# Two raw quads moved into an idle activation buffer, and a newly searched instruction order, in a fused linear-attention and MLP kernel

## The chip, the cores and the metric

One core of a Trainium2 chip. The metric is the device time of one execution in microseconds (us). Runs of one kernel on one chip scatter by 1 to 2 us in either direction, so a difference of 1 us is only seen over several runs of both kernels on the same chip.

## The reference

```python
def phi(x):                                   # x: 8 batches, 8 heads, 576 positions, 64 channels
    proj = einsum('bhsd,md->bhsm', x, omega)  # omega: 128 x 64
    return concatenate([cos(proj), sin(proj)], axis=-1) / sqrt(m)
q_p, k_p = phi(q), phi(k)
kv  = einsum('bhsm,bhsd->bhmd', k_p, v);  z = sum(k_p, axis=2)
num = einsum('bhsm,bhmd->bhsd', q_p, kv); den = einsum('bhsm,bhm->bhs', q_p, z)
x = (num / den), heads side by side           # 8 x 576 x 512
u = x + ((x^T @ U) @ V)^T                     # low rank, over the positions
out = u + relu(u @ w_ch1) @ w_ch2             # 512 -> 2048 -> 512
```

Inputs and output are float32. The kernel computes in bf16 with float32 sums.

## The kernel before

The 64 heads are taken as 16 "quads" of four heads and as 32 "groups" of two. Each head pair's k and q are loaded (`ld/k/n`, `ld/q/n`), transposed (on TensorE for quads 0 to 3: `tpp`, copied out by `tp`, which is called the eviction; by a transposing DMA, also `tp`, for the later quads), multiplied by omega (`ak`, `aq`), turned into table angles on VectorE (`uk`, `uq`), into sines and cosines on ScalarE (`s`, `c`, with a quarter-turn `p` between them on GpSimd), then into `kv` (TensorE, copied by `kvb`), numerators (`num`) and the normalised `x`. The MLP products are `w1` and `w2`. v is loaded (`ldv`) and widened to bf16 on GpSimd (`wv`).

Every instruction is a word of one long list; each engine executes its own words in the order of the list.

```python
rawp = ctx.enter_context(tc.tile_pool(name="rawp", bufs=2))     # two quads of raw k and q
hidp = ctx.enter_context(tc.tile_pool(name="hidp", bufs=2))     # two MLP activation buffers
low_f = hidp.tile([P, NFT, SM], BF16, name="hid")...bitcast(F32)  # the second one, unused until batch 1,
Vf  = low_f[:, 0:S]                                             # is where U and V are staged
U_f = low_f[:, S:S + NS * R]...
# ...
add("gate", DVE, lambda: nc.vector.memset(low_f[:, S - 1:S + NS * R], 0.0))
add("low", SP, load_low_rank, needs=["gate"])                   # four DMAs
add("lowc", POOL, cast_low_rank, needs=["low"])
# ...
def load_w1(a):                                                 # a quarter of W1: 512 KB
    nc.gpsimd.dma_start(W1b[:, a, :, :], moe_w_ch1[:, a * 512:(a + 1) * 512]...)
# ...
    need = [r for r in read_raw(name, n - NRAW)] if n >= NRAW else []   # NRAW = 2
    add(("ld", name, n), POOL, lambda ...: nc.gpsimd.dma_start(load(name, n), quad(src, n)), needs=need)
# ...
    add(("ldv", n), SP if n else POOL, load_v, needs=[("wv", n - 2)] if n >= 2 else [])
    add(("wv", n), POOL, widen, needs=["begin", ("ldv", n)] + ...)
```

The part of the order, with cuts:

```
... ukh/0/1 aq/0@4 d/8@6 gate skh/0/0 uq/0 d/9@7 low ... pk/0 tpp/k/1@6 uk/1 ... ldv/1 pq/0 tp/k/1 d/11@1
aq/1@1 tp/q/1 ld/q/2 cq/0 uq/1 ak/2@3 wv/0 aq/2@6 uk/2 d/12@1 s/1 W1/0 ldv/2 kv/0/0@0 ld/k/3
uq/2 ak/3@2 W1/1 kv/0/1 p/1 ... p/2 num/0 tp/k/2 tp/q/2 d/13@2 sk/3 x/0 ak/4@5 ld/q/3 wv/1 ...
```

## Time and profile before

| | before |
|---|---|
| time, median of 4 fast runs | 358.88 us (358.36 to 359.5) |
| span of the profiled run | 358.0 us |
| TensorE (PE) busy | 341.3 us, 95% |
| PE idle before 30 us | 9.3 us |
| start of the first MLP product that needs W1's second piece | 39.94 us |

PE is the bound from 30 us on. A second profile of the same kernel, taken later on another chip, ends at 356.05 us; below it is "before, second profile".

### The profile page before, as it was taken

What the parts mean: (1) busy time and instruction counts of PE and PEld (TensorE: products, weight loads), DVE (VectorE), ACT (ScalarE), POOL (GpSimd) and SP (SyncE); (2) the same over time, 40 slices, a digit from 0 to 9 for tenths busy, and PEclk for the clock granted to TensorE, in tenths of its full rate; (3) what the DMA queues carried; (4) which work ended last, traced back from release to release, by engine and by line L of the source; (5) the groups of instructions that cost most, each with busy time, mean ns of one, the idle gap of its engine ahead of it and who ended that gap; (6) DMA issues with size and microseconds to landing.
All of it is one profiled execution on the core that took longest, in us unless ns stands there. A gap on an engine that the chain in (4) does not pass through costs nothing.

```text
span 358.0 us, 8213 instructions
## 1 busy us (share of the span) xinstructions
PE 341.3 (95%) x3544; PEld 180.4 (50%) x3585; DVE 193.2 (54%) x284; ACT 216.8 (61%) x223; POOL 117.3 (33%) x100
## 2 busy tenths in 40 slices
PE   7659999999999999989999999999999999999996
PEld 3446456454564554645455554554545544444444
DVE  3968868786687676866476754364320722000111
ACT  5868899559958877678829578437386004553210
POOL 5879185427634536324704043003230000000000
PEclk9869999999999999999999999999999999999999
DMA  8997989999999886999992086200722051511124
GB/s 173 224 239 116 203 142 195 217 178 227 192 194 192 123 246 128 115 177 166 196 183 46 3 212 140 62 3 0 148 60 44 2 104 29 117 31 29 37 53 88
DMA packets 68567, 45.06 MB, mean 126 GB/s; under 512 B 47156, under 2 KB 59828, under 8 KB 68532
## 3 DMA queue, kind: packets, MB, share of 16 engines
q1 hardware_dynamic: 55348, 30.09, 41.2%
q0 software_dynamic: 12816, 13.93, 25.5%
q8 instruction: 28, 0.46, 0.5%
q10 hardware_dynamic: 368, 0.52, 0.4%
q14 instruction: 7, 0.06, 0.1%
HBM read 37.16 MB, written 9.44 MB: 130 GB/s over the span
## 4 chain that ended last, share of the span: by engine, by line
PE 88%; DMA 7%; ACT 1%; issue 1%; POOL 1%; POOLq 0%
PE ps L610 35%; PE ps L630 34%; PE ps L430 5%; PE ps L444 4%; DMA raw<-in_q_dram 4%; DMA T<-raw 3%; PE ps L381 2%; PE ps L407 2%; PE ps L576 2%; PE ps L449 1%; PE ps L514 1%; ACT ft L416 1%; PE ps L321 1%; POOL ang L420 1%; PE ps L584 0%
## 5 line engine op out<-in xcount | busy, mean ns | idle before, releaser
L416 ACT ACTIVATE ft<-ang 128x2304 bf16<-128x2304 int16 (+2 forms) x67 | 134.1, 2020 | 35.4 <-DVE ang L359 15.3
L630 PE MATMUL ps<-W2b,hid 128*128 128x512 bf16 (+1 forms) x560 | 130.5, 373 | 2.6 <-issue 1.4
L623 ACT ACTIVATE hid<-ps 128x512 bf16<-128x512 f32 x144 | 81.9, 596 | 84.4 <-PE ps L610 83.9
L610 PE MATMUL ps<-uT,W1b 128*128 128x512 bf16 x512 | 121.7, 379 | 0.8 <-DMA uT<-u 0.6
L420 POOL TENSOR_SCALAR ang<-ang 128x2304 int32<-128x2304 int32 (+2 forms) x34 | 67.9, 2000 | 126.2 <-ACT ft L416 119.4
L359 DVE TENSOR_SCALAR ang<-ps 128x1280 int32<-128x1280 f32 (+2 forms) x66 | 84.8, 1313 | 24.7 <-PE ps L375 16.3
L630 PEld LDWEIGHTS <-hid 128*128 128x128 bf16 x592 | 55.4, 98 | 62.0 <-issue 2.1
L610 PEld LDWEIGHTS <-W1b 128*128 128x128 bf16 x576 | 54.3, 98 | 63.8 <-issue 1.4
L646 DVE TENSOR_TENSOR o<-ps,u 128x512 f32<-128x512 f32 x32 | 21.9, 686 | 52.1 <-PE ps L630 52.0
L430 PEld LDWEIGHTS <-ft 64*128 64x128 bf16 x1152 | 24.1, 96 | 9.9 <-issue 5.7
L430 PE MATMUL ps<-vq,ft 64*128 64x65 bf16 x1152 | 27.1, 193 | 1.4 <-DVE ang L359 0.9
L460 DVE TENSOR_TENSOR x<-ps,rec 128x640 bf16<-128x640 f32 x32 | 26.4, 825 | 1.1
L434 DVE CAST kvb<-ps 128x260 bf16<-128x260 f32 x32 | 13.4, 423 | 20.6 <-PE ps L430 19.8
L578 DVE TENSOR_TENSOR u<-ps,x 128x1024 bf16<-128x1024 f32 x16 | 19.2, 1221 | 9.6 <-PE ps L610 4.9
L305 POOL CAST vq<-vraw 128x1152 bf16<-128x1152 f32 x16 | 18.5, 1153 | 12.1 <-DMA vraw<-in_v_dram 12.1
L444 PEld LDWEIGHTS <-ft 128*128 128x128 bf16 x512 | 19.9, 99 | 5.0 <-issue 0.5
L444 PE MATMUL ps<-kvb,ft 128*128 128x65 bf16 x512 | 21.9, 195 | 0.0
L610 PE MATMUL ps<-utailT,W1b 128*128 128x512 bf16 x64 | 15.1, 379 | 0.0
L458 DVE RECIPROCAL ps<-ps 128x10 f32<-128x10 f32 x32 | 7.2, 224 | 13.8 <-PE ps L449 13.3
L381 PE MATMUL ps<-WT,T 64*128 64x128 bf16 x256 | 13.5, 222 | 1.1 <-DMA T<-raw 0.6
L298 POOL DMA_DIRECT2D raw<-in_k_dram x15 | 10.9, 725 | 10.2 <-ACT hid L623 6.3
L407 PE MATMUL ps<-T,WT 64*128 64x512 bf16 x64 | 13.2, 387 | 0.0
(58 smaller groups left out, 150.7 us busy)
## 6 DMA issues: line engine op xcount, KB each, us to landing
out_dram<-o SPq DMA_DIRECT2D x70, 128.0 KB, 2.4
vraw<-in_v_dram SPq DMA_DIRECT2D x15, 576.0 KB, 5.7
raw<-in_k_dram POOLq DMA_DIRECT2D x15, 288.0 KB, 5.7
raw<-in_q_dram POOLq DMA_DIRECT2D x15, 288.0 KB, 6.0
W1b<-in_moe_w_ch_dram POOLq DMA_DIRECT2D x4, 512.0 KB, 9.9
W2b<-in_moe_w_ch_dram POOLq DMA_DIRECT2D x4, 512.0 KB, 8.9
vraw<-in_v_dram POOLq DMA_DIRECT2D x1, 576.0 KB, 7.5
ang<-in_q_dram ACTq DMA_DIRECT2D x1, 288.0 KB, 3.5
```

The lines of the kernel that those rows point to most:

```text
L359: nc.vector.tensor_scalar(out=dst, in0=src, scalar1=TO_UNITS, scalar2=None, op0=ALU.mult)
L381: nc.tensor.matmul(pk[:, e, i * P:(i + 1) * P], kT[r, c, :], WT[r, :])
L407: nc.tensor.matmul(pq[:, e, :], WT[r, :], transposed("q", n)[r, c:c + 4, :])
L416: nc.scalar.activation(out=held["ft", g].rearrange("p f a c -> p f (a c)")[:, f, lo:hi], in_=low[:, lo:hi, 0], func=ACT.Sin, scale=TO_RAD)
L420: nc.gpsimd.tensor_scalar(out=ang, in0=ang, scalar1=TURN / 4.0, scalar2=1.0, op0=ALU.add, op1=ALU.mult)
L430: nc.tensor.matmul(kv_ps[:, hh, o], ft[r, f, 0, c:c + M], vq[n % NV][r, NS * (g % 2) + s, :], start=(s == 0), stop=(s == NS - 1))
L444: nc.tensor.matmul(nd[:, hh, t, :], ft[:, f, 1, c:c + P], kvb[:, hh, f, :], start=(f == 0), stop=(f == 1))
L460: nc.vector.tensor_tensor(out=x[:, :, hp * P:(hp + 1) * P].rearrange("p t (h d) -> p h t d", h=2), in0=nd[:, :, :, 0:D], in1=rec.unsqueeze ...
L610: nc.tensor.matmul(one(key), W1b[:, f // 4, ct, f % 4 * P:(f % 4 + 1) * P], uT[:, :, ct, :], start=(ct == 0), stop=(ct == NCT - 1))
L623: nc.scalar.activation(out=held["hid", b][:, f, :], in_=one(at_bank), func=ACT.Relu)
L630: nc.tensor.matmul(one(key)[:, 0:cs.stop - cs.start], held["hid", b][:, f, t * P:(t + 1) * P], W2b[:, f, cs], start=(f == 0), stop=(f == N ...
L646: nc.vector.tensor_tensor(out=held["o", b, t][:, cs], in0=one(key)[:, 0:cs.stop - cs.start], in1=u[:, t, cs], op=ALU.add)
```

## The change

The stated intent: keep the first two raw quads in the second MLP activation buffer, so that the loads of quads 2 and 3 need not wait for the transposes of quads 0 and 1, and search the whole order again with later transfers assumed late and with loads kept apart from DMA transposes.

```diff
+    low_h = hidp.tile([P, NFT, SM], BF16, name="hid").rearrange("p f t -> p (f t)")
+    low_f = low_h.bitcast(F32)
+    early_raw = [low_h[:, 2 * (S + NS * R) + n * 4 * NS * D:...].rearrange(...) for n in range(2)]
...
-            held["raw", n] = rawp.tile([P, 2, 2, NS * D], BF16, name="raw")
+            held["raw", n] = early_raw[n] if n < 2 else rawp.tile([P, 2, 2, NS * D], BF16, name="raw")
...
-                need = [r for r in read_raw(name, n - NRAW)] if n >= NRAW else []
+                need = [r for x in "kq" for r in read_raw(x, n - NRAW)] if n >= NRAW + 2 else []
...  (batch 1's activations wait for the transposes of quads 0 and 1)
```

The order, cut (the new one; all other words move as well):

```
begin first/k/0 first/k/1 ident first/q/0 om ld/k/0 ... ld/q/0 d/2@5 ldv/0 ... ld/k/1 ... ld/q/1 ... ld/k/2 ... W1/0
... ld/q/2 ... wv/0 skh/0/0 ukh/0/1 ... ld/k/3 ld/q/3 ... pk/0 ... tp/k/1 tpp/k/2@0 tp/q/1 pq/0 d/10@5 gate tp/k/2
ak/2@5 low ... ldv/1 kv/0/1 ldv/2 ... p/1 num/0 tp/q/2 x/0 p/2 c/1 aq/3@0 ak/4@5 uq/3 aq/4@2 ld/k/4 ... lowc
... ld/q/4 uk/5 sq/3 pk/3 ... x/1 d/12@5 wv/1 ... pq/3 ck/3 ldv/3 kv/2/0@0 ... wv/2 ... p/4 ... x/3 ut0/0 ut0x/1@0 ut0/1 W1/1
```

## The prediction

> **What bounds the kernel now.** I read the busy table first, then the 40 slices, the chain that ended last, the waits of each engine in the first 40 us, and a table of windows.
>
> ```profile
> PE 341.3 (95%) x3544; PEld 180.4 (50%) x3585; DVE 193.2 (54%) x284; ACT 216.8 (61%) x223; POOL 117.3 (33%) x100
> PE   7659999999999999989999999999999999999996
> PEclk9869999999999999999999999999999999999999
> DMA  8997989999999886999992086200722051511124
> PE 88%; DMA 7%; ACT 1%; issue 1%; POOL 1%; POOLq 0%
> ```
>
> TensorE (PE) is the bound, at nine tenths or more in every slice (8.95 us each) but the first three, one in the middle and the last. The change does not alter the number of matmuls, so time can come only from PE's lost time, 358.0 - 341.3 = 16.7 us idle, plus what it loses at half clock. The windows place it:
>
> ```profile
> 0.00:4.57 4.57, 3.21 (x8) 1.16 (x9) 0.52 (x5) 2.24 (x4) 3.82 (x11) 1.00 0.61 160
> 4.57:14.81 10.24, 6.85 (x79) 3.67 (x78) 8.47 (x14) 6.90 (x9) 4.99 (x6) 1.00 1.05 213
> 14.81:25.05 10.24, 6.70 (x97) 5.33 (x98) 7.02 (x10) 6.68 (x4) 8.32 (x8) 0.50 1.17 235
> 25.05:30.00 4.95, 3.90 (x146) 3.25 (x142) 4.79 (x8) 4.89 (x5) 4.37 (x6) 1.00 0.76 129
> 30.00:100.00 70.00, 69.48 (x888) 37.83 (x892) 53.54 (x80) 57.48 (x56) 39.32 (x33) 1.00 1.07 187
> 100.00:200.00 100.00, 97.35 (x1213) 52.67 (x1228) 69.28 (x97) 69.28 (x61) 40.45 (x30) 1.00 0.90 156
> ```
>
> The second number is the length, the third PE's busy time, the last three the clock, the DMA share and GB/s. Before 30 us PE is idle 1.36 + 3.39 + 3.54 + 1.05 = 9.3 us, and runs 10.24 us at half clock. From 30 us on it idles 0.5 us to 100, 2.65 us to 200 and little after. So the opening is what a load change can win. In it, the chain and the waits show
>
> ```profile
> 11.84 1.20 POOL ang L420
> 13.03 8.91 DMA raw<-in_q_dram
> ...
> 21.99 1.14 PE ps L321 x9
> 23.13 0.88 PE ps L444 x16
> ...
> 24.27 3.29 ACT ft L416 x2
> PE ps L321 <- DMA raw<-in_q_dram: 3.6, 3, 2.6
> ACT ft L416 <- PE ps L449: 2.9, 1, 2.9
> ```
>
> The load of q for quad 2 is issued only at 13.03, because its raw buffer is that of quad 0, and lands 8.9 us later. PE stands before its transposes (L321), and behind them in PE's order is the first numerator (L444, L449). ScalarE (ACT) waits 2.9 us for that numerator before its next sine, and VectorE (DVE) 2.8 us for the transposes. That is the stall the change aims at.
>
> **What the Trainium skill says.** "DMA: Bandwidth & Descriptors", section "Issuing engines are not separate DMA queues": transfers started by any engine run on the same 16 DMA engines and interleave. The trace agrees: 235 GB/s and a DMA share of 1.17 while that load took 8.9 us, against 4.0 us for the quickest load of this kind. An earlier issue moves such a load ahead of others but makes no bandwidth. "TensorE: Matmul & The Clock Gate", Part 1: the clock is either half or full, and recent activity decides. The trace agrees that it is binary (0.50 or 1.00); here the half state lasted 10.24 us, longer than the 3.4 us window that the page states. The same DMA page, section "Rules for kernel authors", says to issue loads early and wait late, which is this change's idea.
>
> **The change part by part.** (a) Quads 0 and 1 go to the still unused second activation buffer, so both rotating raw buffers are free for quads 2 and 3. Their loads lose the wait for the transposes of quads 0 and 1. In exchange, batch 1's activations (r/1) wait for those transposes, which are done some 60 us before; that costs nothing. (b) GpSimd (POOL) now issues v/0 third, then quad 1, k/2, the first quarter of W1, and q/2 at once. Nine issues at about 0.72 us each from 1.44 end near 7.1, so q/2 is issued near 6.5 instead of 13.0. (c) The second quarter of W1 moves from 16.3 us to behind the quarter-turn of group 4; the low-rank loads and v/1, v/2 move behind the evictions of quad 1. (d) The evaluation of group 5 is brought forward. (e) The 20 dummy matmuls stay, but 13 instead of 16 lie in the opening, seven at the end, behind the last real matmul. (f) All the rest of the order is searched again.
>
> When does q/2 land? All bytes before it on its queue still count. Quads 0 and 1 together have 1152 KB in bf16, of which half-quads of 144 KB come from the first loads: 864 KB on this queue, then v/0 576, k/2 288, W1 512, q/2 288: 2528 KB. The busiest of the early windows moved 213 to 235 GB/s, and the first 608 KB come from other queues, so 3136 KB at about 220 KB/us from 2 us gives 16 us, plus a tail of 1 to 2 us, and some more for v/1: **17 to 19 us**, 3 to 5 us before the 21.94 of now.
>
> Is that worth 3 us? No: I walked the new order of each engine with durations of the forms in the first 40 us. DVE: angle conversions of 1280 columns 1.48 us, of 1024 columns 1.20, eviction of a half quad (1152 columns) 0.75, kv copy 0.42, normalisation 0.22 + 0.17 + 0.82. From the end of the second quarter conversion at 8.73: uk/1, ut/0, uq/0, uq/1, two evictions, the gate, one eviction, uk/2, uq/2, kvb/0 and uk/3 sum to 11.4 us, so 20.1. Then q/2's eviction, x/0, uq/3, uk/4, kvb/1, uq/4, uk/5, x/1, uq/5, kvb/2, kvb/3, k/3's eviction, two hu copies, x/2 and x/3 sum to 14.8, so x/3 ends near 34.9, or 34 as neighbouring records overlap a little. Now it ends at 34.39. So DVE, without gaps, replaces the load as the bound: x/3 comes no earlier, but the 2.7 us of group 5's conversions are done before it, and so are PE's products for group 5 (0.33 + 0.05 + 0.32 us in the chain).
>
> ACT agrees. The first quarter-turn on POOL now stands behind the widening of v/0 (1.15, after v/0 lands near 8.5 to 10) and two issues, so it starts near 11.2 instead of 9.66. The first cosine, first q sine and q cosine then end near 17, s/1 and s/2 (2.12 each) near 21, c/1 and c/2 near 25.3, against 27.6 now; sk/3, sq/3 (1.27, 1.05) near 27.6, s/4 29.7, ck/3 and cq/3 near 32, against about 31 now, but with s/4 done.
>
> PE's gain I read at the first MLP product that needs the second quarter of W1 (w1/0/4). Now it starts at 39.94. In the new order it follows x/3 by the chain of a small product, copy, product, eviction, 1.6 us, and some seven 0.22 us products: near 38. One product pair of 0.43 us, done later now, is by then done too. Gain up to 39.9 + 0.4 - 38.1 = **2.2 us**. Against it: W1's second quarter, issued near 33 behind two widenings and the quarter-turns. A quarter of W1 landed 7.6 us after issue at best in this trace, so 40 us or more. With less traffic then (that part of the trace was busy) I take 39 to 40: it gives back about 1 us. Opening: **-1.2 us**.
>
> Later: between 100 and 200 us PE waits 1.2 us for a transposing DMA (0.6 for uT, 0.6 for T). An order that keeps loads away from them may save most; I count **-0.7 us**. End: seven dummies of 0.22 us beside the last addition and store: 0. Sum: 358.8 - 1.2 - 0.7 = 356.9.
>
> **The rivals.** *The load is truly the bound, and 4 us go with it.* For: the chain gives it 8.9 us, and ACT and DVE both idle nearly 3 us behind it. Against: DVE is busy 5.00 of 5.00 us from 10 to 20, and the widening of v/0 delays ACT by a microsecond and more. Time: 354 to 355. *A new wait on weights.* For: W1's second quarter leaves its early place, and 7.6 to 12.7 us from issue to landing is measured. Against: the search was told to assume late transfers. With a 3 us wait: 358 to 360. *Loads hidden anyway, the rest saturated.* PE is at 0.99 from 30 us on, so an opening that reaches the same x/3 at the same time saves only the work done in its gaps: 357 to 358.5. *The clock.* If the half state falls after 25 us, where PE is saturated, it costs up to 5 us: 362. Against: PE does more real work in the window before, and as little activity as today's brought the full clock back at 25.05.
>
> **Range and chances.** The centre leans to the small gain of my sum: 356.8 us. The low end, 353.6, is the first rival with all middle waits gone; the high end, 360.4, a weight wait and some loss in the middle. 2% is 7.2 us: to be faster by that, three quarters of the opening's idle time would have to go; I give it 0.04. Slower by that needs a long weight wait and a half clock together: 0.02.
>
> **What would show it.** Right: the wait of L321's counterpart for q under 1 us; q/2 landing before 19.5; ACT no longer waiting 2.9 us for a numerator; DVE busy over 4.7 in each 5 us from 10 to 30; x/3 between 33.5 and 35.5; PE waiting for W1 up to 2 us near 38 to 40. Wrong: x/3 before 33 (then the load was the bound), a wait for W1 over 3 us, a half-clock stretch that reaches past 26 us, or new waits of PE for transposing DMAs after 100 us.

## The result, and the profile after

Lines of the changed kernel have numbers higher by 3: L321 became L324, L359 became L362, L416 L419, L420 L423, L444 L447, L449 L452, L610 L613.

| | before | changed |
|---|---|---|
| time, median of 4 fast runs | 358.88 us (358.36 to 359.5) | 359.99 us (359.78 to 361.01) |
| ratio | | 1.0036, 95% interval 1.0011 to 1.0061 |

A ratio is the mean time of one kernel's fast runs over that of the other's in the same rounds, so it is not quite the ratio of these medians. Five more rounds on another chip gave 1.0029 (0.9994 to 1.0063) for the changed kernel and 0.9995 for the kernel before against itself. The change costs about 1 us; a small gain had been forecast.

The busy table, PE's slices, the clock and the DMA share of the changed kernel's page, and its chain by engine:

```profile
PE 344.7 (96%) x3550; PEld 181.9 (51%) x3585; DVE 193.7 (54%) x284; ACT 218.2 (61%) x223; POOL 117.2 (33%) x100
PE   7779899999999999999999999999999999999997
PEclk9768999999999999999999999999999999999999
DMA  8998999899979996893096947432701135111124
PE 86%; POOL 4%; DMA 4%; issue 2%; DVE 1%; ACT 1%; POOLq 0%; ACTq 0%; DVEq 0%
```

In PE's row only the opening looks different; of the chain, POOL holds 4% instead of 1, and DMA 4% instead of 7. The same stretches as in the prediction, for the changed kernel:

```profile
14.81:25.05 10.24, 7.17 (x136) 5.71 (x132) 9.27 (x11) 8.78 (x5) 6.08 (x4) 0.67 1.04 225
25.05:30.00 4.95, 4.73 (x51) 2.98 (x50) 4.88 (x8) 4.95 (x5) 4.61 (x6) 0.50 0.78 123
30.00:100.00 70.00, 67.50 (x924) 37.45 (x930) 49.84 (x77) 52.30 (x52) 35.78 (x31) 1.00 1.04 184
100.00:200.00 100.00, 98.88 (x1169) 52.47 (x1179) 65.88 (x89) 72.35 (x65) 39.80 (x31) 1.00 0.76 149
```

Three things are to be seen. Before, the half clock was one stretch, 14.81 to 25.05 us, where PE was idle a third of the time. Now it is two, 13.43 to 20.26 and 23.67 to 30.50 us, and the second falls where PE is full: from 25.05 to 30 us it is busy 4.73 of 4.95 us at 0.50. From 30 to 100 us PE now lacks 2.5 us instead of 0.5. And from 100 to 200 us it lacks 1.1 instead of 2.65. PE's waits over the first 100 us:

```profile
PE ps L613 <- DMA W1b<-in_moe_w_ch_dram: 1.7, 1, 1.7
PE ps L324 <- DVE ang L362: 1.7, 3, 0.8
PE ps L384 <- DVE ang L362: 1.5, 2, 0.8
```

The wait of 2.6 us for the raw q is gone, so the change does what it was made for. A wait of 1.7 us for W1 has come. The milestones, from the starts and ends of single instructions in the traces (x/n is the end of the normalisation of group n; "ready" is the start of the first MLP product that needs W1's second piece):

| us | before | before, second profile | changed | changed, second profile |
|---|---|---|---|---|
| x/0 | 25.56 | 25.05 | 21.94 | 21.90 |
| x/1 | 30.14 | 29.63 | 29.28 | 28.93 |
| x/2 | 32.20 | 31.70 | 34.01 | 34.04 |
| x/3 | 34.39 | 33.89 | 35.20 | 35.24 |
| ready | 39.94 | 39.44 | 42.53 | 42.07 |
| end | 357.96 | 356.05 | 359.23 | 358.56 |

(Some of the expectations below count x/3 from another zero, 0.24 us earlier: their 35.5, 35.4 and 32.9 are 35.24, 35.14 and 32.62 here.)

x/0 comes 3.6 us earlier; by x/2 all of that and 2 us more is lost. From "ready" to the end three of the four profiles take nearly the same: 316.6 us (before, second), 316.7 and 316.5 (changed); the first profile of before takes 318.0, with 1.2 us of waits for transposing DMAs, which its second profile does not show. So the result is made before 43 us: +2.6 us there, and 1.3 us back in the middle, which is the stall of before that comes and goes.

### The profile page after: what moved, and what is told of

The parts are those of the page before. It is cut to its first block, busy times and chain, and to the rows that moved or that the text cites. A ratio compares the mean times of both kernels' runs of the same rounds, so it can differ in the third digit from the quotient of the medians.

```text
span 359.2 us, 8219 instructions
## 1 busy us (share of the span) xinstructions
PE 344.7 (96%) x3550; PEld 181.9 (51%) x3585; DVE 193.7 (54%) x284; ACT 218.2 (61%) x223; POOL 117.2 (33%) x100
## 4 chain that ended last, share of the span: by engine, by line
PE 86%; POOL 4%; DMA 4%; issue 2%; DVE 1%; ACT 1%; POOLq 0%; ACTq 0%; DVEq 0%
PE ps L613 34%; PE ps L633 34%; PE ps L433 5%; PE ps L447 4%; POOL ang L423 2%; DMA W1b<-in_moe_w_ch_dram 2%; PE ps L384 2%; PE ps L410 2%; DMA vraw<-in_v_dram 2%; PE ps L579 2%; ACT ft L419 1%; DVE ang L362 1%; PE ps L452 1%; PE ps L517 1%; POOL vq L308 1%
## 5 line engine op out<-in xcount | busy, mean ns | idle before, releaser
L419 ACT ACTIVATE ft<-ang 128x2304 bf16<-128x2304 int16 (+2 forms) x67 | 133.5, 2020 | 37.3 <-DVE ang L362 22.3
L633 PE MATMUL ps<-W2b,hid 128*128 128x512 bf16 (+1 forms) x560 | 132.0, 373 | 2.7 <-issue 1.6
L626 ACT ACTIVATE hid<-ps 128x512 bf16<-128x512 f32 x144 | 83.1, 597 | 74.2 <-PE ps L613 72.1
L613 PE MATMUL ps<-uT,W1b 128*128 128x512 bf16 x512 | 119.8, 379 | 1.7 <-DMA W1b<-in_moe_w_ch_dram 1.7
L423 POOL TENSOR_SCALAR ang<-ang 128x2304 int32<-128x2304 int32 (+2 forms) x34 | 67.9, 1998 | 121.0 <-ACT ft L419 111.1
L362 DVE TENSOR_SCALAR ang<-ps 128x1280 int32<-128x1280 f32 (+2 forms) x66 | 85.3, 1316 | 28.0 <-PE ps L378 13.5
L613 PEld LDWEIGHTS <-W1b 128*128 128x128 bf16 x576 | 54.6, 98 | 66.1 <-DMA W1b<-in_moe_w_ch_dram 2.2
L433 PEld LDWEIGHTS <-ft 64*128 64x128 bf16 x1152 | 22.7, 96 | 8.6 <-issue 6.5
L581 DVE TENSOR_TENSOR u<-ps,x 128x1024 bf16<-128x1024 f32 x16 | 19.4, 1222 | 13.6 <-PE ps L579 11.9
L433 PE MATMUL ps<-vq,ft 64*128 64x65 bf16 x1152 | 25.8, 194 | 0.9 <-DVE ang L362 0.7
L447 PEld LDWEIGHTS <-ft 128*128 128x128 bf16 x512 | 20.4, 100 | 5.6 <-issue 0.9
L447 PE MATMUL ps<-kvb,ft 128*128 128x65 bf16 x512 | 22.2, 197 | 0.2 <-DVE kvb L437 0.2
L410 PE MATMUL ps<-T,WT 64*128 64x512 bf16 x64 | 13.6, 393 | 1.1 <-DVE x L463 0.5
L613 PE MATMUL ps<-utailT,W1b 128*128 128x512 bf16 x64 | 14.5, 379 | 0.0
L384 PEld LDWEIGHTS <-T 64*128 64x128 bf16 x256 | 8.8, 97 | 10.4 <-issue 9.3
```

What stands on the lines that cost most here:

```text
L362: nc.vector.tensor_scalar(out=dst, in0=src, scalar1=TO_UNITS, scalar2=None, op0=ALU.mult)
L384: nc.tensor.matmul(pk[:, e, i * P:(i + 1) * P], kT[r, c, :], WT[r, :])
L419: nc.scalar.activation(out=held["ft", g].rearrange("p f a c -> p f (a c)")[:, f, lo:hi], in_=low[:, lo:hi, 0], func=ACT.Sin, scale=TO_RAD)
L423: nc.gpsimd.tensor_scalar(out=ang, in0=ang, scalar1=TURN / 4.0, scalar2=1.0, op0=ALU.add, op1=ALU.mult)
L433: nc.tensor.matmul(kv_ps[:, hh, o], ft[r, f, 0, c:c + M], vq[n % NV][r, NS * (g % 2) + s, :], start=(s == 0), stop=(s == NS - 1))
L447: nc.tensor.matmul(nd[:, hh, t, :], ft[:, f, 1, c:c + P], kvb[:, hh, f, :], start=(f == 0), stop=(f == 1))
```

## The experiments

Eighteen kernels were run, all correct. Each edits the order by moving words; a diff shows the neighbourhood. "Changed buffers" means that the new buffers are kept while the order is that of before. Ratios are to the kernel before on the same chip.

### The two kernels again

No edit.

> The kernel before, unchanged, as a measure of the noise and for a profile on the same chip as the others. Every theory: ratio 0.998 to 1.002. What is open is whether the stall of 1.4 us of PE near 155 us, which the first profile of before has behind transposing DMAs and which no variant with that order showed, is in this profile too.

> The changed kernel, unchanged, for a profile and times on this chip. Expected: 1.003 to 1.006 of before, a wait of PE for the second quarter of W1 of 1 to 2 us near 42 us, x/3 ended at 35 to 35.5.

Measured: 358.53 us, ratio 0.9995 (0.9955 to 1.0035), and 360.06 us, 1.0029 (0.9994 to 1.0063). The loss repeats in size. The stall of before in the middle does not.

### The buffers alone, and the one load alone

```diff
 # b_reloc: the new buffers, the order of before
 # b_reloc_q2: besides
-... ld/k/2 tp/q/0/0 ...   aq/1@1 tp/q/1 ld/q/2 cq/0
+... ld/k/2 ld/q/2 tp/q/0/0 ...   aq/1@1 tp/q/1 cq/0
 # b_q2_mid: ld/q/2 right behind pk/0 instead
```

> The changed kernel's buffers (quads 0 and 1 in the second activation buffer, no wait of the loads of quads 2 and 3) with the order of the kernel before. Theory (the buffers alone do nothing, as the load of q for quad 2 still stands behind two quarter-turns in GpSimd's order and is issued near 13.0): wait of L324 for q of 2 to 3 us stays, 0.998 to 1.002 of before. Rival (the wait on the buffer was itself the cause): the wait falls below 1 us and the time to 0.995 or less.

> As b_reloc, and the load of q for quad 2 issued right after that of k for quad 2 (near 5.5 us), ahead of the first quarter-turn; everything else in the order of before. Theory (the load was a real bound of this order, and the reordering of POOL and W1 is what lost its gain): q lands before 17, PE's 2.6 us and ACT's 2.9 us waits go, x/3 ends 1 to 2.5 us earlier, 0.993 to 0.997 of before. Rival (as my prediction had it, DVE is the bound as soon as the load is not): x/3 moves by less than 1 us and the time is 0.997 to 1.000 of before.

> As b_reloc_q2, but the load of q for quad 2 is issued between the two quarter-turns of group 0 (near 10.8 us, where GpSimd waits for about 1.1 us anyway) and so leaves quad 1's loads more alone. If the wait for k of quad 1 (1.9 us in b_reloc_q2, 1.0 in before) comes from the additional early load: it falls to 1.0 to 1.5 us and the time is 0 to 0.5 us below b_reloc_q2's. If q then lands too late: a wait of L324 for q of over 1 us is back and the time is 0.5 to 1 us above it.

Measured: b_reloc 357.59 us, 0.9958 (0.9919 to 0.9996); b_reloc_q2 356.40 us, 0.9925 (0.989 to 0.9959); b_q2_mid 356.32 us, 0.9942 (0.9906 to 0.9978). x/3 ends at 33.95, 32.62 and 31.81 us, the profiles at 356.11, 354.75 and 354.10.

The buffers alone leave the stall: q of quad 2 is issued at 12.76 us (12.91 in before's second profile), behind the second quarter-turn in GpSimd's order, and PE still waits 2.4 us for it. That b_reloc is 0.4% faster was not expected; its trace ends as before's second profile does (356.05), so this is not explained and may be scatter. The single load, moved into the order of before, is worth 1.3 us at x/3 against b_reloc in b_reloc_q2 and 2.1 us in b_q2_mid, and 1.4 and 2.0 us at the profiles' ends; in median time b_reloc_q2 is 1.2 us below b_reloc, and buffers and load together are 2.1 us below before. PE's wait for k of quad 1, 1.9 us in b_reloc_q2, is 0.9 in b_q2_mid, as expected; the two times cannot be told apart. **These two kernels beat the kernel before and the changed one**. So the load of q for quad 2 did set the pace of the old order. The loss comes from the newly searched order.

### The late piece of W1

```diff
 # a_w1_early, on the changed kernel
-p/2 c/1 aq/3@0 ak/4@5 uq/3 aq/4@2 ld/k/4 c/2 ...   x/3 ut0/0 ut0x/1@0 ut0/1 W1/1 ut0x/2@5
+p/2 c/1 aq/3@0 ak/4@5 uq/3 aq/4@2 ld/k/4 W1/1 c/2 ...   x/3 ut0/0 ut0x/1@0 ut0/1 ut0x/2@5
 # b_w1_late, on the kernel before: W1/1, W1/2 and W1/3 behind p/4
```

> The changed kernel with one word of its order moved: the second quarter of the first MLP weight (W1/1) is issued right after the load of k for quad 4 (near 24.3 us) instead of after the quarter-turn of group 4 (34.4 us). Theory (the weight wait took what the opening had won): the 1.7 us wait of the L613 matmul is gone, w1/0/4 starts near 40.8 instead of 42.5, and the time falls by 1.5 to 2 us against the changed kernel, to 0.995 to 0.998 of before. Rival (the half-clock stretches and POOL's detour cost the time, the weight only seems to): less than 0.5 us is won, 1.002 to 1.004 of before.

> The kernel before with the last three quarters of the first MLP weight issued after the quarter-turn of group 4, as the changed kernel has them (issue near 35.0 us), nothing else changed. Theory: w1/0/4 waits for the second quarter until about 42, so PE loses 1.5 to 3 us there: 1.003 to 1.008 of before. Rival (such a wait is made up elsewhere because PE waits less later): 0.998 to 1.002.

Measured: a_w1_early 359.06 us, 1.001 (0.9974 to 1.0045). PE's wait for W1 is gone, "ready" is at 40.73 instead of 42.07 us, the end at 357.21 instead of 358.56. The mirror, b_w1_late, took 360.07 us, 1.0037 (0.9999 to 1.0074), with "ready" at 40.08, 0.64 us later than in before's second profile. The late piece is worth about 1 us, about the whole loss against the kernel before. It does not explain x/3, nor why the gain of the one load is not there.

### VectorE's work taken away ahead of x/3

The prediction held that VectorE, without gaps, sets x/3. In a_g5_late (with W1 early) the four angle and feature steps of group 5 move behind x/3 (its sine and some low-rank steps of batch 0 move along); b_q2_g5 does the reverse to b_reloc_q2, from here on called the good order.

```diff
 # a_g5_late
-kvb/1 ak/5@5 uq/4 ... ld/q/4 uk/5 sq/3 ... s/4 aq/5@2 x/1 ... tpp/k/3@5 uq/5 hu0/1@7
+kvb/1 uq/4 ... ld/q/4 sq/3 ... s/4 x/1 ... tpp/k/3@5 hu0/1@7          (and all four behind x/3)
```

> The changed kernel with W1's second quarter early (as a_w1_early) and the evaluation of group 5 (two PE products, two DVE conversions of 1.48 and 1.20 us, its sine and cosine) put back behind x/3 and its evictions. If DVE's work ahead of x/3 is what keeps x/3 late: x/3 ends 1.5 to 2.7 us earlier than in a_w1_early (35.4), near 33 to 34, w1/0/4 starts 0.5 to 2 us earlier, and the time falls to 0.995 to 0.999 of before. If ACT and POOL (cosines, widening of v/1) hold x/3: x/3 moves by less than 0.7 us and the time by less than 0.5 us against a_w1_early.

> The best variant so far (b_reloc_q2) with group 5's products and conversions put ahead of x/2, as the changed order has them. If DVE's work ahead of x/3 matters: x/3 ends 1.5 to 2.7 us later than 32.9, and the time is 0.3 to 1.5 us longer than b_reloc_q2's (PE has 0.7 us of the work done earlier). If not: x/3 within 0.7 us and the time within 0.5 us of b_reloc_q2.

Measured: a_g5_late 364.83 us, 1.0183 (1.0152 to 1.0213): slower, since group 5 then gets in the way of batch 0 (PE waits 3.2 us after x/3, 2.3 of them for VectorE). The point of the run is x/3: 35.08 us, against 35.14 in a_w1_early. Taking 2.7 us of VectorE work away moves it by nothing. The waits in its first 36 us, of all engines, show what held it:

```profile
DVE kvb L437 <- PE ps L433: 2.7, 1, 2.7
PE ps L433 <- POOL vq L308: 0.9, 1, 0.9
```

VectorE simply waits those 2.7 us for PE's kv of groups 2 and 3, and PE waits for GpSimd's widening of v for quad 1. So "VectorE is the bound of x/3" falls for the changed order. In b_q2_g5, 359.98 us, 1.0042 (1.0018 to 1.0066), the extra work does delay x/3, to 37.06 us. That is 4.4 us, more than the 2.7 us of VectorE's work, and half clock lies there from 28.31 to 35.13 us; the run does not tell the two apart.

### ScalarE's first quarter-turn

```diff
 # a_pk_first
-... skh/0/1 d/9@7 ld/k/3 ld/q/3 aq/0@6 ut/0 aq/1@0 pk/0 uq/0
+... skh/0/1 d/9@7 aq/0@6 ut/0 aq/1@0 pk/0 ld/k/3 ld/q/3 uq/0
 # a_both: a_pk_first with W1/1 behind ld/k/4
```

> The changed kernel with the loads of k and q for quad 3 issued after the first quarter-turn instead of before it (two issues of 0.72 us less ahead of ACT's first cosine). If ACT's delay is what keeps x/3 late: the first cosine starts near 11.1 instead of 12.5, x/3 ends 0.8 to 1.4 us earlier, and with it the issue of W1's second quarter, so the time falls by 0.8 to 1.4 us. If DVE is the bound, as my prediction said: x/3 moves by less than 0.5 us and the time by less than 0.5 us.

> The changed kernel with both edits: quad 3's loads after the first quarter-turn, and W1's second quarter right after the load of k for quad 4. If the two delays are the whole loss of the changed order: 0.993 to 0.997 of before. If DVE bounds x/3: as with the weight alone, 0.998 to 1.002 of before.

Measured: 360.42 us, 1.0046 (1.0007 to 1.0084), and 360.30 us, 1.0038 (1.0002 to 1.0074). A miss: ScalarE starts 1.1 us earlier, x/3 ends at 34.61 and 35.21 us, and no time is gained. But one line of a_both is worth keeping, PE's longest wait from 20 to 36 us:

```profile
PE ps L433 <- POOL vq L308: 1.5, 1, 1.5
```

Here PE was ready for the kv of groups 2 and 3 1.5 us early, and again it was v that came too late.

### v earlier in the changed order

The chain of waits of the changed kernel's second profile, from VectorE's eviction of quad 1 to W1's second piece (start, length, what), says why the widening of v is late:

```profile
14.66 0.30 DVE hid L246
...
16.98 8.09 DMA hid<-in_moe_U_dram
...
25.23 0.42 POOL Ub L250
...
27.75 1.27 POOL ang L423
29.02 0.57 POOL vq L308
...
32.20 2.03 POOL ang L423
34.22 7.80 DMA W1b<-in_moe_w_ch_dram
42.07 1.04 PE ps L613 x4
```

The gate's memset (L246) now stands behind VectorE's evictions of quad 1. SP cannot issue the low-rank loads before it, and v/1 and v/2 stand behind those in SP's order: SP's row for the low-rank V starts at 14.99 us in the changed kernel and at 8.95 in before. GpSimd then waits 1.3 us for U, and everything behind it shifts: the turn of group 3, v's widening (28.96 us; 21.84 in before), W1. The first try moved only the widening:

```diff
 # a_wv1_early: a_w1_early, and
-num/0 tp/q/2 x/0 p/2 c/1 ...   x/1 d/12@5 wv/1 hu0/0@4
+num/0 tp/q/2 x/0 p/2 wv/1 c/1 ...   x/1 d/12@5 hu0/0@4
```

> The changed kernel with W1's second quarter early and the widening of v/1 moved ahead, right behind the quarter-turn of group 2 (from about 29.1 to about 23.6 us). If POOL's queue holds the kv products of group 2 and through them x/2 and x/3: x/2 starts 2 us or more earlier and x/3 ends 1 us or more earlier than 35.4. If DVE is the bound: x/3 moves by less than 0.7 us.

Measured: 363.57 us, 1.0154 (1.0129 to 1.0178); GpSimd waited 2.7 us for v/1, which had not landed, and x/3 fell back to 38.62 us. So the load had to be moved, not the widening. Three runs did this: the gate back in its earlier place in the changed order, alone and with the other two moves, and the gate moved late in the good order.

```diff
 # a_gate, on the changed kernel
-... wv/0 skh/0/0 ukh/0/1 ak/1@3 ...   pq/0 d/10@5 gate tp/k/2 ak/2@5 low kv/0/0@2
+... wv/0 skh/0/0 ukh/0/1 gate low ak/1@3 ...   pq/0 d/10@5 tp/k/2 ak/2@5 kv/0/0@2
 # a_gate_wv1_w1: besides wv/1 behind p/2 and W1/1 behind ld/k/4
 # b_q2_gate_late, on b_reloc_q2: gate, low and ldv/1 behind tp/q/1
```

> The changed kernel with one edit: the gate memset and the low-rank loads behind it go back to where the order before has them, right behind the first group's head transposes of k. Gate theory (in the changed order the gate stands behind VectorE's evictions of quad 1, so SP cannot issue the low-rank loads until about 15 us, SP's loads of v/1 and v/2 stand behind them, and POOL then waits 1.3 us for U on its way to pk/3, wv/2, p/4 and the issue of W1): the low-rank loads are issued at 8.8 to 9.5 us instead of 15.0, v/1 and v/2 near 11.5 to 13 instead of 17.6, POOL's wait for U is gone, x/2 and x/3 end 1 us or more earlier than the 34.3 and 35.5 of the changed kernel, W1's second piece is issued 1 us or more earlier than 34.2, and the time is 1 to 2 us lower: 0.997 to 1.000 of before. Rival (POOL's own order binds, or the early low-rank loads only push q/2 and k/1 back): x/3 moves by under 0.5 us and the time stays at 1.002 to 1.005 of before.

> The gate back in its earlier place, and besides wv/1 right behind p/2 and W1's second piece issued right behind the load of k/4. The same two moves without that of the wv/1 run's late v/1 cost 1.5 per cent (a_wv1_early, 1.0154): POOL waited 2.7 us for v/1. Gate theory (v/1 was late because SP's load of it stood behind the gate): no wait for v/1 at wv/1, kv/2 2 us or more earlier than 30.2, x/3 at 34.0 or below, no wait of the first MLP matmuls for W1, 0.992 to 0.997 of before. Rival (v/1 is late for the DMA queues' sake, or POOL's order has no room for wv/1 there): POOL still waits over 1.5 us, 1.010 or more of before.

> The mirror: the relocated buffers with the order before and q/2's load moved up (0.9925 of before), and the gate, the low-rank loads and the loads of v/1 and v/2 moved behind the evictions of quad 1, as the changed order has them. Gate theory: the low-rank loads land some 5 us or more later, the casts and wv/1 on POOL are late, x/3 ends 1 to 3 us later than the 32.9 of the run without this move, and the time is 1 to 3 us longer: 0.995 to 1.001 of before. Rival (the gate's place is free): x/3 within 0.5 us of 32.9 and 0.991 to 0.994 of before.

Measured: a_gate 361.16 us, 1.0058 (1.0033 to 1.0084); a_gate_wv1_w1 363.68 us, 1.0139 (1.011 to 1.0168); b_q2_gate_late 359.19 us, 1.0012 (0.9989 to 1.0036). The profiled run of a_gate fell in a slow state, near half clock throughout (588.5 us), so it has only its times. The mirror held: in the good order the late gate costs 0.9% (1.0012 against 0.9925, timed on different chips, each ratio known to 0.2 to 0.35%), x/3 goes from 32.62 to 35.02 us, and PE stands 3.3 us before the same line. GpSimd's and PE's waits there are one thing, as PE's from 20 to 36 us shows:

```profile
PE ps L433 <- POOL vq L308: 3.3, 1, 3.3
```

In the changed order, however, the early gate gained nothing. PE's longest waits in a_gate_wv1_w1 (first 100 us) say why:

```profile
PE ps L384 <- DMA T<-raw: 2.5, 1, 2.5
PE ps L324 <- DMA raw<-in_q_dram: 2.4, 1, 2.4
```

The wait for q of quad 2, the one that the change removes, is back. Against the changed kernel's second profile, v/1's load is issued 5.5 us earlier (12.15 instead of 17.62) but lands only 1.3 us earlier (24.80 instead of 26.14), and q/2 lands 3.9 us later (20.73 instead of 16.80). The gate alone is not the cause.

### The transfers brought forward

The changed order also issues W1's first piece at 5.5 us, ahead of q/2, and k/3 and q/3 near 10 us. In before they go out at 14.7, 15.5 and 21.1 us. These are 1,088 KB that nobody needs before 25 us. And the DMA engines move no more in all: over the first 30 us, before's second profile, the changed kernel's second and b_reloc_q2's show

```profile
0.00:30.00 30.00, 20.33 (x342) 13.45 (x343) 21.08 (x36) 21.09 (x20) 22.03 (x30) 0.89 0.95 199
```

```profile
0.00:30.00 30.00, 21.91 (x277) 14.07 (x278) 23.16 (x37) 21.45 (x20) 20.71 (x28) 0.84 0.99 197
```

```profile
0.00:30.00 30.00, 23.15 (x361) 15.02 (x362) 22.41 (x40) 22.14 (x21) 23.13 (x31) 0.83 0.96 199
```

The last number is GB/s: 199, 197 and 199, so 5.9 to 6.0 MB each, at a DMA share of 0.95 to 0.99 (the number before). The orders only share out the same bytes. (PE's busy times, the first number after the length, do not measure the work done, as products at half clock take longer.)

```diff
 # a_gate_bytes, on a_gate
-ld/k/2 ... W1/0 omt@2 ...   d/9@7 ld/k/3 ld/q/3 aq/0@6 ...   pq/0 d/10@5 ...   x/0 p/2 c/1
+ld/k/2 ... omt@2 ...   d/9@7 aq/0@6 ...   pq/0 W1/0 ld/k/3 d/10@5 ...   x/0 p/2 ld/q/3 c/1
 # a_gate_bytes_wv1: besides wv/1 behind ld/q/3 and W1/1 behind ld/k/4
 # b_q2_bytes, on b_reloc_q2: W1/0 ahead of ld/q/2, and ld/k/3 ld/q/3 behind pk/0
```

> The changed kernel with the gate and the low-rank loads early (as in the run with the gate alone, 1.0058 of before), and besides the transfers that the new order had brought forward put back: W1's first piece and k/3 behind the second quarter-turn of group 0 (about 15 us, was 5.5 and 9.6) and q/3 behind the quarter-turn of group 2 (about 23 us, was 10.3). Bytes theory (1,088 KB that nobody needs before 25 us stood in the queues ahead of q/2, v/1 and U; with the gate late v/1 and U pay, with the gate early q/2 pays): q/2 lands before 17 us instead of 22.4, v/1 before 21, no wait of TensorE for q/2 over 1 us, x/3 1.5 us or more earlier than 35.5, the time 0.995 to 1.001 of before. Rival (the order of POOL's own work binds, not the bytes): x/3 within 0.7 us of 35.5 and 1.002 to 1.007 of before.

> As the run with the gate and the transfers put back, and besides wv/1 right behind q/3's load and W1's second piece right behind the load of k/4. The same two moves without the bytes put back cost 1.4 to 1.5 per cent. Bytes theory: POOL waits under 0.5 us for v/1, x/3 at 33.5 us or earlier, no wait for W1, 0.991 to 0.998 of before. Rival: POOL still waits over 1 us for v/1 or the time is 1.003 or more.

> The mirror: the relocated buffers with the order before and q/2's load moved up (0.9925 of before), gate early as there, and W1's first piece brought ahead of q/2 and k/3, q/3 behind the first quarter-turn, as the changed order has them. Bytes theory: q/2 lands at 19 us or later and v/1 later than 21, TensorE waits 2 us or more for q/2, x/3 1.5 to 4 us later than 32.9, the time 0.998 to 1.010 of before. Rival (the bytes ahead are free): x/3 within 0.7 us of 32.9 and 0.990 to 0.995 of before.

Measured: a_gate_bytes 358.27 us, 1.001 (0.9987 to 1.0032) against 1.0058 with the gate alone: the changed order is mended to the time of before. q/2 lands at 15.38 us, v/1 at 21.11, and W1's second piece is waited for 0.2 us. x/3 is at 34.18 us, 1.1 us earlier than in the changed kernel, where the theory wanted 1.5. b_q2_bytes 358.87 us, 1.0022 (0.9999 to 1.0045): in the good order the same transfers, brought forward, cost 1.0% (against 0.9925, again on another chip). Its longest wait of PE in the first 50 us, and GpSimd's wait for v from 5 to 45 us:

```profile
PE ps L324 <- DMA raw<-in_q_dram: 2.0, 1, 2.0
```

```profile
POOL vq L308 <- DMA vraw<-in_v_dram: 3.8, 1, 3.8
```

q/2 and v/1 both pay: they land at 20.82 and 24.71 us instead of 15.58 and 21.41. The size at x/3, 33.57 against 32.62 us, is below the 1.5 us that had been expected, and "ready" is 1.3 us later. The other 1.1 us at the profile's end lies later, where PE has small waits that b_reloc_q2's profile does not show (0.5 us for a transposing DMA, 1.4 us in nine short gaps); the edit does not explain them. W1's piece and quad 3's loads were not tried apart.

a_gate_bytes_wv1 took 362.42 us, 1.0113 (1.0084 to 1.0141), though v/1 was widened at 23.39 us; x/3 ended at 34.83. It lost time twice. First, PE waits 2.9 us after x/3 for a transposing DMA, and a further half clock follows, from 53.27 to 56.68 us. The transpose of quad 4 is issued at 30.86 us in a_gate_bytes and lands 6.9 us later. Here it is issued at 35.18, behind two loads of weights issued at 33.86 and 34.64, and lands 17.7 us later. The same is seen wherever the transpose is issued 0.1 to 0.7 us behind a weight load: 18.0 us in a_gate_wv1_w1, 17.9 in a_wv1_early, 13.6 in b_w1_late. In the other fast profiles it lands within 6.9 to 10.4 us. So keeping loads apart from DMA transposes, which the search was told to do, fits the runs, though none moved a transpose alone. Second, x/3 did not profit from v/1, for the reasons that follow.

### Which of two bounds holds x/3 in the changed order

No engine explains x/3 alone. Windows of 3.41 us show the second bound. They are cut 0.24 us after the clock changes, so 0.97, 0.96 and 0.54 each hold a bit of the neighbouring state. The changed kernel, second profile (start:end length, PE busy, then the other engines, clock, DMA share, GB/s):

```profile
20.84:24.25 3.41, 1.81 (x50) 1.19 (x50) 3.00 (x5) 3.20 (x3) 3.10 (x3) 0.97 1.03 232
24.25:27.67 3.42, 2.75 (x33) 1.81 (x32) 3.42 (x5) 3.42 (x4) 2.44 (x4) 0.50 0.84 163
27.67:31.08 3.41, 3.31 (x69) 2.36 (x69) 2.52 (x6) 3.03 (x2) 3.38 (x5) 0.54 0.71 93
```

and b_reloc_q2:

```profile
14.85:18.27 3.42, 2.00 (x50) 1.18 (x49) 3.42 (x4) 3.02 (x3) 3.25 (x5) 0.96 0.98 270
18.27:21.68 3.41, 2.53 (x30) 2.50 (x29) 3.37 (x5) 3.41 (x2) 3.00 (x2) 0.50 1.16 236
21.68:25.10 3.42, 3.34 (x64) 2.37 (x61) 3.01 (x5) 2.92 (x3) 3.42 (x4) 0.54 1.22 210
```

In both, a window in which PE is busy 1.8 to 2.0 us is followed by two at half clock. In the good order they are over at 24.9 us. In the changed order PE has done its early work by 20.8 us, is thin until 24.25, and meets the half clock with its kv, its numerators and the transposes of quad 3 in front of it: from 25 to 30 us it is busy 5.00 of 5.00 us at 0.50. As an estimate, that is 2.9 us of full-speed work: the first sixteen products of a numerator take 0.87 us there (from 25.65) and 0.51 us at full clock (from 31.70). Two dummy products (26.74 and 27.83) take 1.1 us of it; no run removes them. The nineteen fast profiles sort by this: of the seven with no half clock between 26 us and x/3, six end x/3 by 33.95 us (the seventh is before's first profile, 34.39); the twelve with one end it at 34.18 us or later. But ten of the twelve have the changed order and all seven the old one, so they sort by order nearly as well.

That is a correlation, and a late clock is partly the consequence of waits (in b_q2_gate_late it follows PE's wait of 3.3 us). What the runs show of the cause is the following. In the changed kernel PE reaches the kv of groups 2 and 3 at 30.16 us without a recorded wait, and v/1's widening ended at 30.11. The two bounds end together. Where the half clock ended earlier (27.6 us in a_both, 28.6 in a_w1_early), PE waited for v, 1.5 and 0.6 us, and x/3 stayed at 35.2 and 35.1. Where v was widened earlier (23.4 us in a_gate_bytes_wv1), PE did not wait for v, worked at half clock without a gap until 29.4 us, and x/3 came at 34.8. Take one away and the other is there. In that last run there is a third, as its line shows:

```profile
PE ps L433 <- ACT ft L419: 0.5, 1, 0.5
```

ScalarE's cosine of k for group 3 came late, behind a quarter-turn on GpSimd that the moved widening and weight load had pushed from 26.48 us (a_gate_bytes) to 28.46.

No run takes both away from the changed order, so how much of the gap to b_reloc_q2 (x/3 34.18 against 32.62 us even in a_gate_bytes) is the clock alone stays open. No run sets the clock. Nor do the parts add up: the late gate (0.9%), the early transfers (1.0%) and the late piece of W1 (about 0.4%) make more than the 1.0 to 1.1% between the changed kernel and the good order, so they overlap, and no run shows by how much.

## Why the prediction was wrong

The forecast was 356.8 us, a gain of 2; the measured 359.99 is a loss of 1. It lies in the range, the direction is wrong.

- **The bound of PE, and where time can come from**: right. Everything was decided before 43 us.
- **The aimed stall goes**: right. q/2 is issued at 6.22 us and lands at 17.07, as forecast (6.5, and 17 to 19), though the "nine issues" are eight; PE no longer waits for it, and x/0 comes 3.6 us earlier. One reading was wrong: q/2 was not issued late "because its raw buffer is that of quad 0". b_reloc frees the buffer and issues it at 12.76 us; its place in GpSimd's order, behind the second quarter-turn, held it.
- **"So DVE, without gaps, replaces the load as the bound: x/3 comes no earlier"**: this step failed. The end of x/3 was near (34 to 34.9 forecast, 35.20 measured), but by luck: VectorE has gaps (busy 4.27 of 5.00 us from 20 to 25, against the 4.7 that was to show it right), and a_g5_late takes 2.7 us of its work away and x/3 stays. The bounds are v/1, behind the late gate in SP's and GpSimd's order, and PE's half clock. The first rival, "The load is truly the bound", was right for the order of before, though not in size: with the load moved alone x/3 comes 1.3 to 2.1 us earlier, not 4.
- **Part (c), "the low-rank loads and v/1, v/2 move behind the evictions of quad 1"**: seen in the change, then given no cost. In the good order it costs 0.9% (b_q2_gate_late). Part (b), W1's first piece and two more loads early, was counted only as bytes ahead of q/2; in the good order it costs 1.0% (b_q2_bytes).
- **From x/3 to the MLP product**: mis-sized. "A small product, copy, product, eviction, 1.6 us, and some seven 0.22 us products" makes the 3.2 us from 34.9 to 38.1. PE in fact has 5.6 us of work there without a gap (a_w1_early, 35.14 to 40.73), and the kernel before takes 5.55 (34.39 to 39.94). The interval could have been read from the trace of before; this alone turns the 2.2 us gain at that point into nothing.
- **W1's landing**: the new wait was foreseen as a rival and as about 1 us. It is 1.7 us (1.2 in the second profile): the piece is issued at 34.36 us and lands 8.1 us later, at 42.5, not at 39 to 40.
- **The clock rival**: "If the half state falls after 25 us, where PE is saturated" is what happened (23.67 to 30.50 us). The argument against it, more real work before, held only to 20.3 us: from 20.26 to 23.67 PE is busy 1.71 us.
- **Middle and end**: -0.7 and 0 forecast. The middle shows no waits for transposes after 100 us; but before's second profile has none either, so that is a stall that comes and goes, not a gain to count on. The dummies at the end cost nothing: from the start of the last product to the end 4.05 us against 3.92.

In numbers, at "ready": 38.1 forecast without a wait, plus 0.3 for x/3 (35.2 instead of 34.9), 2.4 for the path behind it (5.6 instead of 3.2, without the wait) and 1.7 for W1 make the 42.5 measured, 2.6 us later than before instead of 1.2 earlier. The path is the largest term.

## What to carry to other kernels

When the DMA engines are full, an earlier load is a later one of something else: list what each moved transfer pushes back and which engine's queue stands behind it, before counting the gain. Two bounds that end at the same time hide each other, so removing either alone shows nothing; a run in which a wait takes exactly the place of what was removed is the sign. And try the one aimed move alone in the old order first: here it was the gain, and the new search around it the loss.

## What the Trainium skill lacked or had wrong

- "DMA: Bandwidth & Descriptors", section "Rules for kernel authors", says to issue a DMA early and wait late. It lacks the price when the engines are full: 197 to 199 GB/s over the first 30 us in three orders, whatever was issued first, and 1,088 KB issued 5 to 11 us earlier made PE wait 2.0 us for q/2 and GpSimd 3.8 us for v/1 (b_q2_bytes, 1.0% slower than without).
- The same section says, where it tells which transposes must be kept in order, that one next to ordinary DMAs needs nothing. For the result that holds here (all runs are correct). That row says nothing of the time: the same transpose landed 6.9 to 10.4 us after its issue in fifteen fast profiles, and 13.6 to 18.0 us in the four in which a weight load had been issued 0.1 to 0.7 us ahead.
- "TensorE: Matmul & The Clock Gate", Part 1, gives a window of about 3.4 us. The runs agree: half-clock stretches were 3.41, 6.83, 10.24 or 13.65 us long. It lists the half state for idle windows, tells of a kernel that kept falling into it through short gaps, and gives no busy share that brings or ends it. Counted in 3.41 us windows from the clock's changes, the nineteen fast profiles show 34 full-clock windows in front of half clock, with PE busy 0.5 to 2.4 us; but windows busy 1.7 to 2.4 us were also followed by full clock, so busy time alone does not bring it. The end is sharper: the 25 half-clock windows that were followed by another had PE busy 2.85 us or less, the 34 that were the last 2.96 us or more.
- No page tells of a whole execution near half clock: one of six runs of a_gate took 588.5 us at a mean clock of 0.558, recorded as 0.50 and 0.555 in turn, the other five 359 to 362 us.
